# Batch 2's channel sums on GpSimd, and U and V narrowed in four places of the order

## The chip, the cores and the metric

The kernel runs on one core of a Trainium2 chip. The metric is the device time of one execution in microseconds; of several executions the median is given. The profile is of one execution; its span is the time from its first to its last instruction, and some microseconds lie outside it. The engines are TensorE (PE, with its weight loads PEld), VectorE (DVE), ScalarE (ACT), GpSimd (POOL) and SyncE (SP), which issues most of the DMAs. Each engine takes its own instructions in order.

## The reference

Attention over 4 batches of 12 heads (448 positions, 64 channels) with normed queries and keys, then two MLP layers on the 768 channels of all heads. The first layer norms its input over the channels, the second adds a product with two low-rank factors U and V.

```
def _attn_ref(q, k, v, g_q, g_k):
    q_n, k_n = (rmsnorm(q, g_q), rmsnorm(k, g_k))
    scores = np.matmul(q_n, k_n.transpose(0, 1, 3, 2)) / np.sqrt(q.shape[-1])
    scores = scores - np.max(scores, axis=-1, keepdims=True)
    attn = np.exp(scores)
    attn = attn / (np.sum(attn, axis=-1, keepdims=True) + 1e-09)
    return np.matmul(attn, v)

def _moe_ref(x, g_ln, w_ch1, w_ch2):
    mu = np.mean(x, axis=-1, keepdims=True)
    var = np.mean((x - mu) ** 2, axis=-1, keepdims=True)
    xn = (x - mu) / np.sqrt(var + 1e-06) * g_ln
    return x + np.maximum(xn @ w_ch1, 0.0) @ w_ch2

def _moe2_ref(x, U, V, w_ch1, w_ch2):
    h = x.transpose(0, 2, 1) @ U @ V
    u = x + h.transpose(0, 2, 1)
    return u + np.maximum(u @ w_ch1, 0.0) @ w_ch2
```

## The kernel before

The program has two parts, attention and MLP. Attention goes head by head, 48 heads in all; numbers of heads here count through the batches, so that batch 2 holds heads 24 to 35, and two neighbouring heads make a pair. In one turn of its loop several heads are in different phases: head n's scores (`sc`, matmuls L491 and L492 into `ps`, ScalarE's exponential L494 gives `p`), the product with the values one head behind (`pv`, L509, or L512 to L514 for the parts that are split into a high and a low half, into `po`), the row maxima two heads ahead (`mx`, matmul L455 into `pm`, VectorE's L456 gives `m`, ScalarE's L461 writes it into `ql`), the transposes of the next keys and queries (`t1`, L434 from `kk` into `pk`, copied to `a` at L437; L442 from `qd` into `pq`, copied to `bq` at L445), and the transposes of `ql` (`t2`, L469, copied to `t` at L471, which L492 reads). `kk`, `qd` and `ql` of a pair come from ScalarE's copies L312 and L315 and GpSimd's subtractions L314 and L317. SyncE's L451 moves a head's keys for the second part of the scores. VectorE's copy L523 takes a head's result to `u`, and two DMAs (L526, L527) put it into `x` and its denominators into `sum`.

A turn has four steps. In each step every task of these phases moves on by one piece, and so does the first task of a list `ln`, in which what doesn't belong to a head stands one after the other: `load_uv` from head 4 on, and after a batch's last head `scale` (loads the denominators with L537, inverts them with ScalarE's L541 and VectorE, and multiplies the six 128x448 tiles of `x` with them at L564), `ln_stats` and `ln_apply`, the norm over channels. After batch 2 come `scale`, `ln_stats` and, for the MLP's first weights, `early` and `late`, which load (`wr`), narrow (L71 and L79 on ScalarE, L83 and L87 on VectorE, result `wf`) and split weights (L945 on ScalarE, L946 on GpSimd) during the last heads. So batch 2's norm is worked on beside heads 41 to 47. The order that the program gives is rearranged by a scheduler that places instructions by times it reckons; instructions in `pin` stay in the order of the program among themselves.

`narrow` (L90 to L93) turns a 64-bit-wide input into float32: `scaled` and `bits` (ScalarE, L79 and L71), `join` and `sign` (VectorE, L83 and L87), each for every half in turn. `load_uv` (L113 to L133) calls it at L124 for U and then for V, each loaded by SyncE in two halves (L121), and then splits the factor (L127 and L129, L131 and L132).

`ln_stats` (L153) sums the six tiles of a batch over channels with four VectorE reductions of 112 columns each (L163), takes the mean over the 128 partitions with a matmul by a constant (L169), copies it to `mu` (L172), subtracts it from each tile on GpSimd (L184), squares on ScalarE (L187), adds on VectorE (L181) and takes the variance with a second matmul (L192).

The MLP follows: 4 runs (layer, pair of batches) over the columns of the weights, matmuls L1120, L1242 and L1298, each set in its order by a planner with its own costs.

Of the kernel before, what the change touches and what calls it, by code (L numbers as in the profile page):

```python
# [47 lines left out]
def build(tc, qkv, gg, g_ln, w1a, w2a, w1b, w2b, u_in, v_in, out):  # L48
    nc = tc.nc
    V, A, PL, PE = nc.vector, nc.scalar, nc.gpsimd, nc.tensor  # L50
    with ExitStack() as es:
# [37 lines left out]
        def narrow(raws, f):  # L89
            n = f.shape[1] // len(raws)  # L90
            for op in (scaled, bits, join, sign):
                for i, r in enumerate(raws):
                    op(r, f[:, i * n:(i + 1) * n])  # L93


        A.preload_act_table_set("natural_log_exp_and_others")
        ident = const([P, P], F32, "ident")
# [16 lines left out]
        def load_uv():  # L114
            for src, n, rows in ((u_in, NC * 4 * R, CP), (v_in, S, 4 * R)):
# [7 lines left out]
                yield  # L123
                narrow(parts, f)  # L124
                yield
                if rows == CP:
# [23 lines left out]

        lns, side = {}, {}

        def ln_stats(b, pool=None):  # L153
# [5 lines left out]
            lag = 2 if pool else 1  # L159
            xs = lt("xs")  # L160
            for c in range(NC):
                cs = slice(c * CP, (c + 1) * CP)
                V.tensor_reduce(xs[:, cs], x[b][:, :, cs].rearrange("p k n -> p n k"), AX.X, ALU.add)  # L163
                yield
            yield
            if pool:
                yield
            pm = side["ln"] if pool else bank("mu")
# [57 lines left out]
        def attention(ap, ep, ep2, early, late):  # L226
# [302 lines left out]

            def scale(b, q, h0, h1, pool=None):  # L530

# [21 lines left out]
                lag = 3 if pool else 2  # L553
                for n in range(len(ks) + lag):
                    if n < len(ks):
                        k = ks[n]
                        rs[k] = (f32(pool)[:, n, :] if pool else
                                 lpool.tile([P, S], F32, tag="lt", name=f"r{b}_{k}"))
                        for j in range(2):
                            q.dma_start(rs[k][j * D:(j + 1) * D, :],  # L560
                                        d[2 * k + j:2 * k + j + 1, :].to_broadcast([D, S]))
                    if n >= lag:
                        k = ks[n - lag]
                        pin(V.tensor_tensor(x[b][:, k, :], x[b][:, k, :], rs[k], ALU.mult))  # L564
                    yield
# [9 lines left out]
            for i in range(-3 - T1, NH + 2):  # L575
# [17 lines left out]
                if i - 2 in (H, 2 * H, 3 * H):  # L593
                    b = (i - 2) // H - 1
                    ln.append(scale(b, nc.sync, 0, H, xl[b] if b < 2 else None))
                if i - 2 in (H, 2 * H):
# [918 lines left out]
```

## Time and profile before

| | us |
| --- | --- |
| median of 3 runs (lowest, highest) | 1677.04 (1676.89, 1685.16) |
| the profiled execution | 1676.77 |
| its span | 1674.5 |
| TensorE busy | 1659.7 (99%) |
| VectorE busy | 1218.4 (73%) |
| ScalarE busy | 1003.2 (60%) |
| GpSimd busy | 1087.7 (65%) |
| the core's mean granted clock of TensorE | 0.997 |

The busy time of a pipelined TensorE doesn't tell that it works at its best, so the table is read for what is near its end and not for what is left. In a timeline each line has the start in us from the span's start, the duration, the engine, the line of the kernel, what is written and read, shapes, and the count where several of one kind were put together; in brackets the idle time before it and what ended it. The granted clock is a share of 2.4 GHz, so 0.5 is 1.2 GHz.

### The profile page before, as it was taken

Reading aid. Unit: us, or ns where it says so; the run is one execution under the profiler, and the core shown is the slowest. Engines: PE = TensorE matmul, PEld = TensorE weight load, DVE = VectorE, ACT = ScalarE, POOL = GpSimd, SP = SyncE. Lnnn points to the kernel's source line nnn. Section 1 sums busy time; section 2 is a strip of 40 time slices with the busy share of each in tenths; the row PEclk is TensorE's granted clock in tenths of the full one; section 3 lists DMA queues with packets and bytes.
Section 4 is the critical chain, followed back from the end, with each engine's and each line's share of the span. In section 5 each row is a group of like instructions: output and inputs, shape, how many; then the busy total and the mean of one; then the engine's idle time right before and its main releaser. Section 6 shows DMA issues by size and latency. Waiting matters only on the chain.

```text
span 1674.5 us, 24807 instructions
## 1 busy us (share of the span) xinstructions
PE 1659.7 (99%) x8251; PEld 1442.0 (86%) x8251; DVE 1218.4 (73%) x1941; ACT 1003.2 (60%) x2105; POOL 1087.7 (65%) x963
## 2 busy tenths in 40 slices
PE   8999999999999999999999999999999999999999
PEld 6676666589999999999999999999999999999998
DVE  6878787879887887866767686667667854565665
ACT  6888888767878866554544455444445534454541
POOL 5788767449767787755555587555555655776752
PEclk8999999999999999999999999999999999999999
DMA  3444445776755566544444427565657463443432
GB/s 97 117 100 116 120 117 138 200 223 199 243 173 178 180 212 200 187 141 134 152 133 158 162 83 257 187 219 179 224 192 246 169 207 116 149 151 123 149 125 76
DMA packets 134432, 273.42 MB, mean 163 GB/s; under 512 B 37280, under 2 KB 57664, under 8 KB 134304
## 3 DMA queue, kind: packets, MB, share of 16 engines
q1 hardware_dynamic: 112252, 265.24, 49.8%
q10 hardware_dynamic: 22052, 6.59, 1.7%
q8 instruction: 66, 1.08, 0.3%
q14 instruction: 62, 0.51, 0.1%
HBM read 178.80 MB, written 81.96 MB: 156 GB/s over the span
## 4 chain that ended last, share of the span: by engine, by line
PE 89%; DMA 3%; DVE 3%; issue 2%; ACT 1%; POOL 1%; SPq 0%; POOLq 0%; DVEq 0%; ACTq 0%
PE bank L1120 34%; PE bank L1298 32%; PE bank L1242 6%; PE po L509 4%; PE b L1120 2%; PE b L1242 2%; PE ps L491 2%; PE pm L455 2%; PE ps L492 1%; DVE m L456 1%; DMA raw<-in_qkv 1%; PE t L987 1%; PE xt L977 1%; PE pk L434 1%; PE pq L442 1%
## 5 line engine op out<-in xcount | busy, mean ns | idle before, releaser
L1298 PE MATMUL bank<-h,w 128*128 128x448 f32 x2655 | 586.4, 366 | 0.3 <-DVE h L1112 0.3
L1298 PEld LDWEIGHTS bank<-h,w 128*128 128x128 f32 x2655 | 497.2, 188 | 40.0 <-DVE h L1112 0.6
L1309 DVE TENSOR_TENSOR x<-x,bank 128x448 f32<-128x448 f32 x450 | 275.9, 616 | 192.9 <-PE bank L1298 188.1
L1120 PE MATMUL bank<-xh,w 128*128 128x448 f32 x1158 | 330.4, 367 | 0.0
L794 POOL TENSOR_TENSOR w<-wf,w 128x384 fp32r<-128x384 f32 x201 | 222.6, 1118 | 131.6 <-ACT w L793 131.5
L794 POOL TENSOR_TENSOR w<-s,w 128x384 fp32r<-128x384 f32 x151 | 173.8, 1154 | 155.3 <-ACT w L793 149.9
L1120 PE MATMUL bank<-T,w 128*128 128x448 f32 x1134 | 251.9, 367 | 0.0
L1120 PEld LDWEIGHTS bank<-xh,w 128*128 128x128 f32 x1158 | 216.9, 188 | 18.1 <-issue 0.8
L1120 PEld LDWEIGHTS bank<-T,w 128*128 128x128 f32 x1134 | 211.9, 188 | 16.8
L1120 PE MATMUL bank<-xl,w 128*128 128x448 f32 x579 | 211.7, 366 | 0.0
L793 ACT CAST w<-s 128x384 fp32r<-128x384 f32 x151 | 77.0, 515 | 178.5 <-PE bank L1120 166.0
L793 ACT CAST w<-wf 128x384 fp32r<-128x384 f32 x201 | 101.5, 514 | 101.2 <-PE bank L1120 82.6
L456 DVE TENSOR_REDUCE m<-pm 112x1 f32<-112x448 f32 x192 | 118.5, 619 | 46.4 <-PE pm L455 45.7
L509 PE MATMUL po<-p,vf 112*66 112x448 f32 x328 | 149.8, 539 | 0.1
L83 DVE SCALAR_TENSOR_TENSOR wf<-wf,raw 128x384 uint32<-128x384 uint32 x180 | 134.2, 752 | 10.4 <-ACT raw L71 3.8
L794 POOL TENSOR_TENSOR w<-raw,w 128x384 fp32r<-128x384 f32 x72 | 81.2, 1145 | 57.2 <-ACT w L793 57.1
L1120 PEld LDWEIGHTS bank<-xl,w 128*128 128x128 f32 x579 | 108.8, 188 | 8.7
L79 ACT ACTIVATE wf<-raw 128x384 f32<-128x384 f32 x180 | 99.3, 553 | 20.7 <-DMA raw<-in_w2a 9.5
L494 ACT ACTIVATE p<-ps 112x448 f32<-112x448 f32 x192 | 104.6, 547 | 6.2 <-PE ps L492 3.5
L1112 DVE SCALAR_TENSOR_TENSOR h<-tm,h 128x448 fp32r<-128x448 f32 x103 | 102.2, 992 | 2.8 <-ACT h L1111 2.1
L71 ACT ACTIVATE raw<-raw 128x384 uint32<-128x384 uint8 x180 | 99.9, 558 | 0.0
L1161 DVE TENSOR_TENSOR tm<-tm,bank 128x448 f32<-128x448 f32 x102 | 63.0, 617 | 47.7 <-PE bank L1120 46.8
(283 smaller groups left out, 2989.5 us busy)
## 6 DMA issues: line engine op xcount, KB each, us to landing
wd<-wf SPq DMA_DIRECT2D x94, 384.0 KB
ws<-w SPq DMA_DIRECT2D x84, 384.0 KB
w<-ws SPq DMA_DIRECT2D x84, 384.0 KB
wf<-wd SPq DMA_DIRECT2D x51, 384.0 KB
raw<-wd SPq DMA_DIRECT2D x48, 384.0 KB
raw<-in_w1b SPq DMA_DIRECT2D x48, 384.0 KB
raw<-in_w2b SPq DMA_DIRECT2D x48, 384.0 KB
raw<-in_w2a SPq DMA_DIRECT2D x44, 384.0 KB
```

Of the source, the lines that this page charges most:

```text
L71: A.activation(r[:, :, 0], r.bitcast(U8).rearrange("p n (t q) -> p n t q", t=2)[:, :, 0, 3], AF.Copy, scale=1.0 / 32, bias=-31.0 / 64)
L83: V.scalar_tensor_tensor(f, f, 3, r[:, :, 0], ALU.logical_shift_left, ALU.bitwise_or)
L456: V.tensor_reduce(m[:, c:c + 1], pm[:CP, :S], AX.X, ALU.max)
L494: A.activation(p, pb[:CP, :S], AF.Exp)
L509: PE.matmul(po[:QW, :S], vf[:, j, c, :], ps[c], start=(i == 0), stop=(i == NC - 1))
L793: job(A, 520, lambda: A.copy(form(key)[0], src()), ins, ("hi",) + key, [key])
L794: job(PL, 1100, lambda: PL.tensor_tensor(form(key)[1], src(), f32(form(key)[0]), ALU.subtract), [("hi",) + key], key, rel=rel)
L1112: soon(V, 700, lambda: V.scalar_tensor_tensor(at(*key)[:, 1], src(), 0.0, f32(at(*key)[:, 0]), ALU.max, ALU.subtract), [("hh",) + key], ke ...
L1120: PE.matmul(out[:, :S], wt[:, k, :], xt[:, k, :], start=(first and n == 0), stop=(last and n == 8), skip_group_check=True)
L1242: PE.matmul(at(*to)[:, :S], wt[:, e, :], xt, start=(m in "13" and n == 0), stop=(n == 2), skip_group_check=True)
L1298: PE.matmul(at(*key)[:, :S], wt[:, e % 3, :], t, start=(n == 0), stop=(n == 3 * G - 1))
L1309: V.tensor_tensor(x[b][:, e, :], x[b][:, e, :], at(*key)[:, :S], ALU.add)
```

## The change

`load_uv` no longer runs `narrow` in one piece. A new `narrowed` yields after each of the four operations, so the four stand in four steps of the loop.

`scale` gets a flag `add`, set for batch 2. From the step after the one that multiplies the third tile of `x`, GpSimd adds the tiles as they come: tiles 0 and 1 and then tile 2 in one step, tiles 3, 4 and 5 in a step each, into `sums[2]`. `ln_stats(2)` takes this sum, leaves its four reductions and its empty steps out, and goes to the matmul for the mean at once. The other batches sum as before.

```
--- before.py
+++ after.py
@@ -93,6 +93,13 @@
                     op(r, f[:, i * n:(i + 1) * n])
 
 
+        def narrowed(raws, f):
+            n = f.shape[1] // len(raws)
+            for op in (scaled, bits, join, sign):
+                for i, r in enumerate(raws):
+                    op(r, f[:, i * n:(i + 1) * n])
+                yield
+
         A.preload_act_table_set("natural_log_exp_and_others")
         ident = const([P, P], F32, "ident")
         make_identity(nc, ident)
@@ -121,8 +128,7 @@
                     nc.sync.dma_start(r, src[:, i * n // 2:(i + 1) * n // 2])
                     parts.append(r)
                 yield
-                narrow(parts, f)
-                yield
+                yield from narrowed(parts, f)
                 if rows == CP:
                     V.tensor_copy(u4.rearrange("p c r -> p (c r)"), f)
                     part = u4[:, :, 2 * R:3 * R]
@@ -148,7 +154,7 @@
             by(V.scalar_tensor_tensor(t, t, -0.5, a, ALU.mult, ALU.mult))
             by(V.scalar_tensor_tensor(y if to is None else to, t, 1.5, y, ALU.add, ALU.mult))
 
-        lns, side = {}, {}
+        lns, side, sums = {}, {}, {}
 
         def ln_stats(b, pool=None):
             def lt(n, pool=None):
@@ -157,14 +163,17 @@
                 return lpool.tile([P, S], F32, tag="lt", name=f"ln{b}_{n}")
 
             lag = 2 if pool else 1
-            xs = lt("xs")
-            for c in range(NC):
-                cs = slice(c * CP, (c + 1) * CP)
-                V.tensor_reduce(xs[:, cs], x[b][:, :, cs].rearrange("p k n -> p n k"), AX.X, ALU.add)
-                yield
-            yield
-            if pool:
-                yield
+            if b in sums:
+                xs = sums.pop(b)
+            else:
+                xs = lt("xs")
+                for c in range(NC):
+                    cs = slice(c * CP, (c + 1) * CP)
+                    V.tensor_reduce(xs[:, cs], x[b][:, :, cs].rearrange("p k n -> p n k"), AX.X, ALU.add)
+                    yield
+                yield
+                if pool:
+                    yield
             pm = side["ln"] if pool else bank("mu")
             pin(PE.matmul(pm[:, :S], ones_m, xs, start=True, stop=True))
             yield
@@ -527,7 +536,7 @@
                 q.dma_start(st["sum", b][h:h + 1, :], u[D:D + 1, :])
                 yield
 
-            def scale(b, q, h0, h1, pool=None):
+            def scale(b, q, h0, h1, pool=None, add=False):
 
                 def fold(d):
                     return d[h0:h1].rearrange("h s -> (h s)").rearrange("(p n) -> p n", p=P)
@@ -551,7 +560,7 @@
                 ks = range(h0 // 2, h1 // 2)
                 rs = {}
                 lag = 3 if pool else 2
-                for n in range(len(ks) + lag):
+                for n in range(len(ks) + lag + add):
                     if n < len(ks):
                         k = ks[n]
                         rs[k] = (f32(pool)[:, n, :] if pool else
@@ -559,7 +568,12 @@
                         for j in range(2):
                             q.dma_start(rs[k][j * D:(j + 1) * D, :],
                                         d[2 * k + j:2 * k + j + 1, :].to_broadcast([D, S]))
-                    if n >= lag:
+                    if add and n >= len(ks) - 1:
+                        if n == len(ks) - 1:
+                            sums[b] = xs = lpool.tile([P, S], F32, tag="lt", name=f"ln{b}_xs")
+                        for k in (1, 2) if n == len(ks) - 1 else (n - lag - 1,):
+                            PL.tensor_tensor(xs, x[b][:, 0, :] if k == 1 else xs, x[b][:, k, :], ALU.add)
+                    if lag <= n < len(ks) + lag:
                         k = ks[n - lag]
                         pin(V.tensor_tensor(x[b][:, k, :], x[b][:, k, :], rs[k], ALU.mult))
                     yield
@@ -592,7 +606,7 @@
                     ln.append(load_uv())
                 if i - 2 in (H, 2 * H, 3 * H):
                     b = (i - 2) // H - 1
-                    ln.append(scale(b, nc.sync, 0, H, xl[b] if b < 2 else None))
+                    ln.append(scale(b, nc.sync, 0, H, xl[b] if b < 2 else None, b == 2))
                 if i - 2 in (H, 2 * H):
                     ln.append(ln_stats(b, ap))
                     ln.append(ln_apply(b, ap))
```

The following pieces show the order on an engine, before and in the changed kernel; lines of the changed kernel are higher by 7 ahead of `ln_stats` and by 9 or 14 behind it.

ScalarE in the 56th to 64th us, heads 6 to 9, before; `f` is what becomes U or V (448: V), `r_0` and `r_1` its two loaded halves:

```order
L437 CAST a_8_973<-pk_968 128x448
L79 ACTIVATE f_942<-r_0_943 128x224
L494 ACTIVATE p_1_992<-ps_989 112x448
L79 ACTIVATE f_942<-r_1_945 128x224
L71 ACTIVATE r_1_945<-r_1_945 128x224
L471 CAST t_6_1003<-pt_998 66x448
L494 ACTIVATE p_2_1017<-ps_1014 112x448
L445 CAST bq_1030<-pq_1025 128x448
L290 ACTIVATE qsq_1_1033<-raw_1_814 112x512
```

The changed kernel at the same heads, from head 7's factor of the maxima, `ql`, on to the copy `kk` of pair 5:

```order
L470 ACTIVATE ql_366<-m_953 112x4
L79 ACTIVATE f_1017<-r_0_1018 128x224
L503 ACTIVATE p_0_1049<-ps_1046 112x448
L71 ACTIVATE r_0_1018<-r_0_1018 128x224
L446 CAST a_9_1063<-pk_1058 128x448
L503 ACTIVATE p_1_1076<-ps_1073 112x448
L480 CAST t_7_1087<-pt_1082 66x448
L503 ACTIVATE p_2_1100<-ps_1097 112x448
L454 CAST bq_1113<-pq_1108 128x448
L503 ACTIVATE p_3_1123<-ps_1120 112x448
L79 ACTIVATE f_1017<-r_1_1020 128x224
L321 CAST kk_1043<-raw_1_654 112x8x64
```

The last three of V's four ScalarE instructions stood between head 8's `a` and head 6's `t`; now two stand behind head 7's `ql`, and the other two beside `kk` and `qd` of pair 5.

TensorE at heads 43 to 45, before, with head 44's transposes in the second row and the mean's matmul not among the rows:

```order
L509 MATMUL po_4333<-p_1_4279,vf_354 66x448
L469 MATMUL pt_4357<-identr,ql_368 66x112 x4
L491 MATMUL ps_4365<-bq_4137,a_43_4090 112x448
L492 MATMUL ps_4365<-t_43_4290,a_362 112x448
L455 MATMUL pm_4370<-a_45_4264,bq_4308 112x448
L509 MATMUL po_4333<-p_2_4297,vf_354 66x448
L442 MATMUL pq_4374<-identr,qd_4244 128x112 x4
L491 MATMUL ps_4382<-bq_4137,a_43_4090 112x448
```

And further on, the mean's matmul of batch 2 one head later:

```order
L455 MATMUL pm_4437<-a_46_4340,bq_4379 112x448
L509 MATMUL po_4403<-p_2_4368,vf_354 66x448
L442 MATMUL pq_4441<-identr,qd_4244 128x112 x4
L169 MATMUL ln_305<-ln_xs,ones_m 128x448
L491 MATMUL ps_4449<-bq_4223,a_44_4177 112x448
L492 MATMUL ps_4449<-t_44_4362,a_364 112x448
```

In the changed kernel, from the same product with the values on:

```order
L518 MATMUL po_4339<-p_1_4282,vf_354 66x448
L478 MATMUL pt_4361<-identr,ql_368 66x112 x4
L178 MATMUL ln_305<-ln_xs,ones_m 128x448
L500 MATMUL ps_4369<-bq_4137,a_43_4090 112x448
L501 MATMUL ps_4369<-t_43_4293,a_362 112x448
L464 MATMUL pm_4374<-a_45_4264,bq_4312 112x448
L518 MATMUL po_4339<-p_2_4301,vf_354 66x448
L451 MATMUL pq_4378<-identr,qd_4244 128x112 x4
```

The mean's matmul (`ln_305<-ln_xs`) stood behind head 47's transposes L442 and now stands behind head 44's L469, 24 places of the list ahead, and reads the sum that GpSimd makes.

GpSimd at the same heads, before, with `ql` of the last pair first:

```order
L317 TENSOR_TENSOR ql_370<-raw_0_3848,qd_4244 112x8x64
L946 TENSOR_TENSOR w_277<-wf_4630,w_277 128x384
L946 TENSOR_TENSOR w_278<-wf_4630,w_278 128x384
L946 TENSOR_TENSOR w_279<-wf_4648,w_279 128x384
L946 TENSOR_TENSOR w_280<-wf_4648,w_280 128x384
L184 TENSOR_TENSOR ln_acc<-x_84,ln_mu 128x448
L184 TENSOR_TENSOR ln_sq_4497<-x_84,ln_mu 128x448
L184 TENSOR_TENSOR ln_sq_4508<-x_84,ln_mu 128x448
L184 TENSOR_TENSOR ln_sq_4521<-x_84,ln_mu 128x448
L184 TENSOR_TENSOR ln_sq_4535<-x_84,ln_mu 128x448
L184 TENSOR_TENSOR ln_sq_4552<-x_84,ln_mu 128x448
```

And in the changed kernel:

```order
L326 TENSOR_TENSOR ql_370<-raw_0_3848,qd_4244 112x8x64
L575 TENSOR_TENSOR ln_xs<-x_84 128x448
L960 TENSOR_TENSOR w_277<-wf_4625,w_277 128x384
L575 TENSOR_TENSOR ln_xs<-ln_xs,x_84 128x448 x3
L960 TENSOR_TENSOR w_278<-wf_4625,w_278 128x384
L575 TENSOR_TENSOR ln_xs<-ln_xs,x_84 128x448
L960 TENSOR_TENSOR w_279<-wf_4649,w_279 128x384
L193 TENSOR_TENSOR ln_acc<-x_84,ln_mu 128x448
```

The five additions (L575) have come in around the first two of the weights' subtractions (L946 before, L960 now), and the mean's subtractions (L184, now L193) have moved ahead of the fourth.

## Rows read from the trace of the kernel before

**Rows 1.** The table of stretches: us, busy us (count) by engine, clock, DMA share, GB/s.

```profile
10.00:16.00 6.00, 3.81 (x31) 3.06 (x29) 5.71 (x12) 5.46 (x13) 2.73 (x3) 0.94 0.35 98
16.00:26.00 10.00, 7.40 (x33) 5.85 (x34) 7.54 (x15) 6.47 (x15) 5.25 (x5) 0.52 0.10 24
...
380.00:1674.00 1294.00, 1291.02 (x6409) 1193.23 (x6407) 921.05 (x1387) 702.14 (x1410) 828.57 (x731) 1.00 0.52 172
```

**Rows 2.** Timeline of TensorE, 60 to 69 us: start, duration, instruction, idle before.

```profile
60.77 0.45 PE L492 MATMUL ps<-t,a 66*112 66x448 f32 x1
61.63 0.46 PE L455 MATMUL pm<-a,bq 128*112 128x448 f32 x1 [0.41 <-ACT bq L445]
...
68.52 0.80 PE L434 MATMUL pk<-identr,kk 112*128 112x112 f32 x4
```

**Rows 3.** Timelines of ScalarE, GpSimd and SyncE (DMA issues), 56 to 66 us.

```profile
59.60 0.40 ACT L79 ACTIVATE f<-r 128x224 f32<-128x224 f32 x1 [1.15 <-DMA r<-in_v]
...
61.05 0.53 ACT L445 CAST bq<-pq 128x448 fp32r<-128x448 f32 x1
...
64.45 1.29 POOL L314 TENSOR_TENSOR kk<-raw,kk 112x512 fp32r<-112x512 f32 x1
...
56.67 0.36 SPq L121 DMA_DIRECT2D r<-in_v  x1
```

**Rows 4.** Timeline of TensorE, heads 43 to 46 and two quiet heads before.

```profile
287.57 0.80 PE L442 MATMUL pq<-identr,qd 112*128 112x112 f32 x4
...
294.00 0.80 PE L442 MATMUL pq<-identr,qd 112*128 112x112 f32 x4
...
306.56 0.73 PE L469 MATMUL pt<-identr,ql 112*66 112x112 f32 x4
307.12 0.41 PE L491 MATMUL ps<-bq,a 128*112 128x448 f32 x1
...
308.19 0.80 PE L442 MATMUL pq<-identr,qd 112*128 112x112 f32 x4
...
316.21 0.80 PE L442 MATMUL pq<-identr,qd 112*128 112x112 f32 x4
316.85 0.99 PE L169 MATMUL ln<-ln_xs,ones_m 128*128 128x448 f32 x2
```

**Rows 5.** Timeline of VectorE, 306 to 315 us.

```profile
306.62 0.61 DVE L564 TENSOR_TENSOR x<-x,r 128x448 f32<-128x448 f32 x1
...
307.62 1.36 DVE L163 TENSOR_REDUCE ln_xs<-x 128x112 f32<-128x672 f32 x1
```

**Rows 6.** Timeline of GpSimd, 301 to 329 us.

```profile
301.02 1.67 POOL L317 TENSOR_TENSOR ql<-raw,qd 112x512 fp32r<-112x512 f32 x1
303.73 2.25 POOL L946 TENSOR_TENSOR w<-wf,w 128x384 fp32r<-128x384 f32 x1 [1.04 <-ACT w L945]
...
310.48 1.01 POOL L946 TENSOR_TENSOR w<-wf,w 128x384 fp32r<-128x384 f32 x1 [1.91 <-ACT w L945]
...
321.01 1.13 POOL L184 TENSOR_TENSOR ln_acc<-x,ln_mu 128x448 f32<-128x448 f32 x1 [0.41 <-ACT ln_mu L172]
...
324.31 4.09 POOL L184 TENSOR_TENSOR ln_sq<-x,ln_mu 128x448 f32<-128x448 f32 x3
```

**Rows 7.** Timelines of TensorE and of ScalarE, 329 to 331 us.

```profile
330.71 0.46 PE L492 MATMUL ps<-t,a 66*112 66x448 f32 x1 [0.65 <-ACT t L471]
...
329.49 0.32 ACT L541 ACTIVATE sy<-ss,tiny 128x28 f32<-128x28 f32 x1 [0.58 <-DMA ss<-sum]
```

**Rows 8.** Timeline of TensorE, the start of the span.

```profile
13.20 0.46 PE L455 MATMUL pm<-a,bq 128*112 128x448 f32 x1 [0.91 <-ACT bq L445]
...
19.21 0.74 PE L434 MATMUL pk<-identr,kk 112*128 112x112 f32 x4 [2.60 <-DVE kk L370]
```

**Rows 9.** Timeline of TensorE, the first MLP matmul and a wait in the MLP.

```profile
338.67 0.71 PE L1120 MATMUL bank<-xh,w 128*128 128x448 f32 x1
...
366.20 2.09 PE L1298 MATMUL bank<-h,w 128*128 128x448 f32 x9 [0.26 <-DVE h L1112]
```

More of the change, by code (lines that the diff above doesn't have):

```diff
@@ L93, in narrow, with narrowed @@
                     op(r, f[:, i * n:(i + 1) * n])
+        def narrowed(raws, f):
+            n = f.shape[1] // len(raws)
+            for op in (scaled, bits, join, sign):
+                for i, r in enumerate(raws):
+                    op(r, f[:, i * n:(i + 1) * n])
+                yield
         A.preload_act_table_set("natural_log_exp_and_others")
@@ L123, in load_uv @@
                 yield
-                narrow(parts, f)
-                yield
+                yield from narrowed(parts, f)
                 if rows == CP:
@@ L149, in rsqrt_newton @@
             by(V.scalar_tensor_tensor(y if to is None else to, t, 1.5, y, ALU.add, ALU.mult))
-        lns, side = {}, {}
+        lns, side, sums = {}, {}, {}
         def ln_stats(b, pool=None):
@@ L159, in ln_stats @@
             lag = 2 if pool else 1
[L160 to L163, printed above, removed]
+            if b in sums:
+                xs = sums.pop(b)
+            else:
+                xs = lt("xs")
+                for c in range(NC):
+                    cs = slice(c * CP, (c + 1) * CP)
+                    V.tensor_reduce(xs[:, cs], x[b][:, :, cs].rearrange("p k n -> p n k"), AX.X, ALU.add)
+                    yield
                 yield
-            yield
-            if pool:
-                yield
+                if pool:
+                    yield
             pm = side["ln"] if pool else bank("mu")
@@ L553, in scale @@
                 lag = 3 if pool else 2
-                for n in range(len(ks) + lag):
+                for n in range(len(ks) + lag + add):
                     if n < len(ks):
@@ L561, in scale @@
                                         d[2 * k + j:2 * k + j + 1, :].to_broadcast([D, S]))
-                    if n >= lag:
+                    if add and n >= len(ks) - 1:
+                        if n == len(ks) - 1:
+                            sums[b] = xs = lpool.tile([P, S], F32, tag="lt", name=f"ln{b}_xs")
+                        for k in (1, 2) if n == len(ks) - 1 else (n - lag - 1,):
+                            PL.tensor_tensor(xs, x[b][:, 0, :] if k == 1 else xs, x[b][:, k, :], ALU.add)
+                    if lag <= n < len(ks) + lag:
                         k = ks[n - lag]
@@ L594, in attention @@
                     b = (i - 2) // H - 1
-                    ln.append(scale(b, nc.sync, 0, H, xl[b] if b < 2 else None))
+                    ln.append(scale(b, nc.sync, 0, H, xl[b] if b < 2 else None, b == 2))
                 if i - 2 in (H, 2 * H):
```

2 lines of the change are left out of this document (1 added, 1 removed).

## The prediction

> **What bounds the kernel now.** I read the page's share of each engine first, then the table of stretches. From 380 us to the end, which is the MLP, TensorE is busy for 1291.02 of 1294.00 us at the full clock [rows 1]; its matmuls stand head to tail, nine of 448 columns in 2.09 us, and the longest wait that the timeline names there is 0.26 us [rows 9]. The order of instructions is the same from there on in both kernels. So the MLP takes what it takes, and what the change can win or lose is the moment at which TensorE is done with the attention, when its first MLP matmul starts, at 338.67 us of the span [rows 9]. The profiled execution took 1676.77 us with a span of 1674.5, so 2.3 us lie around the span; it stands 0.3 us below the median of 1677.04. There the question is where TensorE itself waits, and the timeline of its instructions answers it: each step of a head repeats every few us, so a late start shows as a longer distance between two instructions of the same kind. TensorE takes its instructions in order, hence a matmul that waits holds up all behind it.
>
> **The narrowing of U and V in four places.** Before, the eight instructions of a factor stand nearly in a row on ScalarE and VectorE. The second half of V reaches ScalarE's queue ahead of its data: at 59.60 it has idled 1.15 us for the load that SyncE issued at 56.67, so it took 2.9 us from issue to use [rows 3]. Behind it stands the copy of head 8's transposed queries, `bq`, which comes at 61.05, and TensorE's L455 waits for that: from 60.77 to 61.63 it moves 0.86 us for a matmul that takes up 0.2 us elsewhere (nine in 2.09 us [rows 9]), so 0.65 us are lost [rows 2]. In the changed order V's two L79 stand seven and fourteen places lower, behind `bq`, so this wait goes: −0.65. What is late next? V's second half now stands directly ahead of the copy `kk` of pair 5, on which GpSimd's L314 follows (64.45, 1.29 us [rows 3]), and on that head 10's transposes L434 at 68.52 [rows 2]. V's second load is now issued behind the loads of head 14's pair and into a tile that the first half's last operation (L87) must have read; the first half's operations, now a step apart, end about 63.5 by my estimate from their places among the rows of [rows 3], and with 2.9 us for the load the data are there at 66.4, `kk` at about 67.4 and L314 at about 68.8. TensorE, 0.65 earlier, wants the transposes at 67.9. So a wait of 0.9 takes the place of one of 0.65. Bounds: −0.65, if the load starts as early as before, and +1.5, if VectorE takes one 0.6 us step more on the way; I take 0, between the wait that goes and the one that comes. On SyncE that load holds up head 9's keys (L451) by some 4 us; they are read three heads later, about 19 us by the period below, and this costs nothing. The conversions and subtractions that follow (L127 to L132) feed nothing before the second layer's low-rank product and cost nothing here.
>
> **The sums of batch 2 off VectorE.** Four reductions L163, the first 1.36 us long, stand between the row maxima of heads 45 and 46 [rows 5]. The maxima come late through them, then the copies on ScalarE, then TensorE. The price shows in the period of a head, from one L442 to the next: 6.43 us in a quiet one (287.57 to 294.00) and 8.02 in the one from 308.19 to 316.21 [rows 4]. So without the reductions 8.02 − 6.43 = 1.6 us come back. Not all need come back, since VectorE also keeps other narrowing there: I bound it by −1.6 and −0.8 and take −1.6.
>
> **The sums on GpSimd, and the mean's matmul.** This is the largest term. Five additions of 128x448 now stand on GpSimd behind `ql` of the last pair, which ends at 301.02 + 1.67 = 302.69 [rows 6], with two of the weights' subtractions (L946) between them, three additions after the first and one addition after the second. The mean's matmul, L169, is on TensorE at 316.85 now; in the changed order it stands one head earlier, right behind the four transposes L469 of head 44 (306.56) and ahead of the next scores, L491 at 307.12 [rows 4]. It needs the fifth addition. When is that done? GpSimd has no addition of this form in the trace; the nearest is its subtraction L184, same shape and type, two inputs in SBUF, 1.13 us [rows 6]. L946 takes 1.01 us at 310.48 and 2.25 at 303.73, where VectorE runs instructions with two inputs [rows 6]. All free: 302.69 + 5 x 1.13 + 2 x 1.01 = 310.4. Later L184s, beside VectorE's own two-input work, took 4.09 us for three [rows 6], 1.36 or 0.23 more each. With that for the five additions and 2.25 for the first L946: 310.4 + 1.24 + 1.15 = 312.8. With 2.25 for the second one too: 314.0. I take 312.8, as the additions share GpSimd with L946 and VectorE still narrows weights there. The fifth addition also needs the last product of x with the denominators, L564, at 306.62 + 0.61 [rows 5], which is early enough. So TensorE, in order, stands from 307.1 to about 312.8: +5.7, with +3.3 and +6.9 as the bounds. Behind the waiting matmul stand the scores of head 43, the maxima's products of head 45 and everything after, so nothing of TensorE covers it: ScalarE's exponentials and VectorE's maxima have nothing to read either. No work is added on TensorE, as the matmul is only moved.
>
> The rows show that one form, L946, takes 2.25 or 1.01 us [rows 6]. Behind that the Trainium skill, SBUF — State Buffer, section "SBUF: two separate sides", puts a rule that speaks against sums on GpSimd: GpSimd and a VectorE instruction with two SBUF inputs take one shared pair of ports in turns, each for a whole instruction. By it every piece of VectorE's narrowing would be paid here, and the term would be +6.9, the sum 1.2 more; without it +3.3.
>
> **What goes after it.** At 330.71 TensorE's L492 has idled 0.65 us for a copy that stands on ScalarE behind L541, which waited 0.58 us for the transfer of the denominators (329.49) [rows 7]. That transfer starts with a copy on VectorE, no longer late by the reductions, so I count −0.65, with 0 as the other bound. At the last heads the order on ScalarE now has two exponentials behind a cast of weights; TensorE does not wait there now. Bounds 0 and +2 (about the four casts and two-input steps of 0.5 us that such an exponential would wait for), taken as 0, since TensorE is late by the wait above and the weights are not.
>
> **TensorE's clock.** The stretch table has the granted clock at 1.00 everywhere that I looked but in 10 to 16 us (0.94) and 16 to 26 us (0.52) [rows 1]. Of the two levels, 1.2 and 2.4 GHz, it was thus at the lower for 0.12 x 6 + 0.96 x 10 = 10.3 us, from about 15.3 to 25.6. Before it fell, TensorE waited for its first operands, as 0.91 us before 13.20, and was busy for 3.81 of the 6 us from 10 to 16; 2.60 us before 19.21 followed at the lower level [rows 1, 8]. I found no later wait of that size; the new one of 5.7 us would be longer than any. I therefore count on a fall. While TensorE stands it costs nothing; afterwards it costs half of the time until the clock is back. At the start that was 25.6 − 19.2 = 6.4 us, so 3.2 us is the upper bound and 0 (no fall) the lower; I take +2.0, nearer to the upper, as TensorE is denser here than at the start and may regain the clock sooner.
>
> The Trainium skill, TensorE: Matmul & The Clock Gate, section "HAM oscillation — how this bites in real kernels", has it that a TensorE which idles for long between groups of matmuls falls to its lower clock and pays for it again at each such gap. The trace agrees as far as its only fall goes; by the page the term is not 0.
>
> **The sum.** Narrowing 0; reductions −1.6; wait for the additions +5.7; denominators −0.65; tail 0; clock +2.0: +5.45 us. 1676.77 + 5.45 = 1682.2 for an execution like the profiled one, and with the 0.3 up to the median 1682.5. I say 1682, 0.3% above before. A measurement of this kernel can tell about 0.5%, 8.4 us, from no change, and the forecast lies inside that.
>
> **Rivals.** First, the wait does not become the bound: the additions run in GpSimd's idle time, or the matmul waits only shortly. Then only the gains are left, −0.65 − 1.6 − 0.65 = −2.9, which gives 1674. For it speaks that GpSimd idles 1.04 us before 303.73; against it that even with free durations the sum is done 3.3 us after TensorE asks for it. Chance 0.08. Second, the wait comes, but the clock stays up: 5.7 − 2.25 = +3.45, so 1680. For it: the one fall in the trace came after a stretch of sparse work, not after one wait. Chance 0.25. Third, on the other side, the clock's fall lasts: half speed costs half of its length, so with +3.45 from the rest it decides from a low level of 2 x (8.4 − 3.45) = 9.9 us after TensorE starts again; with the 10.3 us of the start it gives 3.45 + 5.15 = +8.6, so 1685.6. For it: this is the length that the trace has; against it: 3.9 us of that lay before TensorE was back at work. Chance 0.13. Fourth, the change is not felt at all, because the sums arrive where other work stood late anyway: 1677, chance 0.06, against the in-order place of the matmul.
>
> **How the numbers follow.** The forecast, 1682 with 1681 to 1684 about it, has 0.45, the rivals 0.08, 0.25, 0.13 and 0.06, and 0.03 is left for anything else. The range from 1676 to 1687 takes in the second and fourth and most of the third and leaves the first out. Faster by over 0.5% would be below 1668.7: the whole waiting of TensorE around the change is smaller than that, so 0.02. Slower by over 0.5% is the third rival, 0.13, and 0.01 of the rest: 0.14. Within: 0.84.
>
> **What would show it.** In the changed kernel's trace: the mean's matmul (the new L178) with an idle time of 3 to 7 us ended by GpSimd's additions, near 313 us; no reductions of batch 2 on VectorE, and head periods near 6.43 after the wait; a granted clock below 1.00 in the ten us after it; no wait for `bq` near 61 us; the first MLP matmul near 344 us instead of 338.67. I am wrong if the additions are done before TensorE arrives, if the clock does not fall, or if the distance from the first MLP matmul to the end differs from before's 1674.5 − 338.67 = 1335.8 us.

## The result, and the profile after

The changed kernel takes 1690.71 us in the median of 6 runs (1687.57 to 1696.54), the kernel before 1677.41 (1676.89 to 1685.16) in as many: slower by 0.7%, ratio 1.007 with an interval from 1.0047 to 1.0094. The profiled execution took 1691.35 us with a span of 1689.6, so 15.1 us more than before's 1674.5. Some executions of several kernels here run a part of the MLP's matmuls 2% slower, as the last section shows; the profiled one of the changed kernel did not.

Where the time came from is read from one kind of instruction that every head has. The transposes of the queries (L442 before, L451 after) start on TensorE at:

| instruction | before, us | after, us | after − before |
| --- | --- | --- | --- |
| head 8's transposes | 58.55 | 57.88 | −0.7 |
| head 9's | 65.94 | 64.03 | −1.9 |
| head 11's | 78.22 | 84.05 | +5.8 |
| head 44's | 294.00 | 301.10 | +7.1 |
| head 45's | 300.85 | 308.62 | +7.8 |
| head 46's | 308.19 | 324.31 | +16.1 |
| head 47's | 316.21 | 330.74 | +14.5 |
| first MLP matmul | 338.67 | 351.87 | +13.2 |
| last MLP matmul | 1670.66 | 1685.37 | +14.7 |

Two places carry it: 6.5 us where V is narrowed (from −0.7 to +5.8), and 6.8 us around the sums of batch 2 (7.8 to 14.5). Some 2 us came in small steps between, 1.3 went in the last heads, and 1.5 came in the MLP, most of it where one matmul waited for VectorE.

**Where V is narrowed.** TensorE's timeline of the changed kernel from 66 us on has the two waits:

```profile
70.14 0.53 PE L443 MATMUL pk<-identr,kk 112*128 112x112 f32 x4 [2.26 <-POOL kk L323]
...
75.10 0.72 PE L500 MATMUL ps<-bq,a 128*112 128x448 f32 x1 [0.86 <-DVE m L465]
```

The line that answers to [rows 2], L443 for head 10's keys, has idled 2.26 us, where before L434 came at 68.52 without a wait. Behind it, on the other engines (ScalarE, GpSimd, VectorE, SyncE):

```profile
67.78 0.40 ACT L79 ACTIVATE f<-r 128x224 f32<-128x224 f32 x1 [2.19 <-DMA r<-in_v]
...
63.03 1.77 POOL L492 TENSOR_TENSOR xl<-p,xl 112x448 fp32r<-112x448 f32 x1 [1.01 <-DVE xl L491]
...
68.82 1.27 POOL L323 TENSOR_TENSOR kk<-raw,kk 112x512 fp32r<-112x512 f32 x1 [2.02 <-ACT kk L321]
...
63.82 1.23 DVE L87 SCALAR_TENSOR_TENSOR f<-r,f 128x224 uint32<-128x224 uint32 x1
...
69.02 1.32 DVE L83 SCALAR_TENSOR_TENSOR f<-f,r 128x224 uint32<-128x224 uint32 x1 [1.31 <-ACT r L71]
70.37 1.37 DVE L87 SCALAR_TENSOR_TENSOR f<-r,f 128x224 uint32<-128x224 uint32 x1
71.78 1.36 DVE L137 CAST v<-f 128x448 fp32r<-128x448 f32 x1
...
55.20 0.80 SPq L249 DMA_DIRECT2D raw<-in_qkv  x2
...
65.13 0.35 SPq L128 DMA_DIRECT2D r<-in_v  x1
```

The load of V's second half leaves at 65.13, against 56.67 before [rows 3]; ScalarE waits 2.19 us for it, then comes the keys' copy, then GpSimd's L323. The loads of the next pair's keys (L249, at 61.33 before) now go ahead of both of V's, at 55.20. The load of the second half left late since it waits for VectorE's L87 on the first half, which ends at 65.05 (SyncE stands 2.84 us for it until then); that took 1.23 us instead of some 0.4, beside GpSimd's subtraction from 63.03 to 64.80. Afterwards three VectorE instructions, two on the second half and L137, the copy of the whole of V, take 1.3 to 1.4 us each, in step with GpSimd's, and the row maximum behind them is what TensorE waits for at 75.10. The copy has only one input, and yet it is long; before, with GpSimd idle when it started, VectorE's timeline has it as

```profile
62.02 0.38 DVE L131 CAST v<-f 128x448 fp32r<-128x448 f32 x1
```

The stretches of the same time as the long waits, in the changed kernel (columns as in [rows 1]), show the clock:

```profile
66.00:70.00 4.00, 1.89 (x6) 0.47 (x4) 2.69 (x5) 2.22 (x6) 1.98 (x2) 1.00 0.43 115
70.00:74.00 4.00, 3.85 (x21) 2.98 (x21) 3.87 (x5) 3.12 (x10) 2.88 (x3) 0.70 0.51 124
74.00:78.00 4.00, 3.14 (x10) 2.20 (x10) 3.66 (x9) 2.73 (x6) 3.31 (x4) 0.50 0.19 65
78.00:82.00 4.00, 4.00 (x13) 2.41 (x12) 1.74 (x4) 1.75 (x3) 2.90 (x3) 0.52 0.21 47
```

0.70, 0.50 and 0.52: the lower level for 0.6 x 4 + 4 + 0.96 x 4 = 10.2 us, after TensorE had been busy for 1.89 of 4 us.

**Around the sums of batch 2.** TensorE, the changed kernel:

```profile
317.82 0.71 PE L464 MATMUL pm<-a,bq 128*112 128x448 f32 x1 [3.92 <-DVE m L465]
...
320.88 1.86 PE L178 MATMUL ln<-ln_xs,ones_m 128*128 128x448 f32 x2 [0.48 <-POOL ln_xs L575]
```

The long wait, 3.92 us, is not that of the mean's matmul (0.48) but one ahead of it, at the product for head 45's maxima, and it ends with a row maximum of VectorE. VectorE's timeline, and GpSimd's beside it:

```profile
311.34 3.08 DVE L578 TENSOR_TENSOR x<-x,r 128x448 f32<-128x448 f32 x1
314.34 1.48 DVE L87 SCALAR_TENSOR_TENSOR wf<-wr,wf 128x384 uint32<-128x384 uint32 x1
315.75 1.48 DVE L83 SCALAR_TENSOR_TENSOR wf<-wf,wr 128x384 uint32<-128x384 uint32 x1
317.15 0.61 DVE L465 TENSOR_REDUCE m<-pm 112x1 f32<-112x448 f32 x1
...
318.75 0.61 DVE L578 TENSOR_TENSOR x<-x,r 128x448 f32<-128x448 f32 x1
...
308.81 1.66 POOL L326 TENSOR_TENSOR ql<-raw,qd 112x512 fp32r<-112x512 f32 x1
310.43 1.45 POOL L575 TENSOR_TENSOR ln_xs<-x 128x448 f32<-128x448 f32 x1
311.84 1.00 POOL L960 TENSOR_TENSOR w<-wf,w 128x384 fp32r<-128x384 f32 x1
312.80 4.01 POOL L575 TENSOR_TENSOR ln_xs<-ln_xs,x 128x448 f32<-128x448 f32 x3
316.77 1.31 POOL L960 TENSOR_TENSOR w<-wf,w 128x384 fp32r<-128x384 f32 x1
...
319.49 1.33 POOL L575 TENSOR_TENSOR ln_xs<-ln_xs,x 128x448 f32<-128x448 f32 x1 [1.41 <-issue]
```

From 308.81 to 318.08 GpSimd works without a break. Every VectorE instruction with two tensors from SBUF that starts in that stretch is long: the product L578 takes 3.08 us (0.61 in [rows 5]), the narrowing steps L87 and L83 1.48 each. The row maximum, whose one input comes from TensorE's result, takes 0.61 us before and after; it only stands behind them in the queue, and so TensorE waits. The additions themselves take 1.33 to 1.45 us, and L960 1.00, where L946 took 2.25 [rows 6]. So at this place GpSimd was the one that was held before, and VectorE is now. The clock again, in this stretch:

```profile
312.00:318.00 6.00, 2.08 (x10) 1.13 (x11) 6.00 (x5) 1.02 (x3) 5.84 (x5) 0.94 0.31 86
318.00:324.00 6.00, 5.52 (x13) 2.85 (x14) 3.02 (x7) 3.59 (x9) 2.40 (x3) 0.50 0.77 239
```

### The profile page after: what moved, and what is told of

It is laid out like the page before. It is cut to its first block, busy times and chain, and to the rows that moved or that the text cites. A ratio compares the mean times of both kernels' runs of the same rounds, so it can differ in the third digit from the quotient of the medians.

```text
span 1689.6 us, 24810 instructions
## 1 busy us (share of the span) xinstructions
PE 1666.0 (99%) x8251; PEld 1445.3 (86%) x8251; DVE 1226.0 (73%) x1937; ACT 1004.2 (59%) x2105; POOL 1090.3 (65%) x968
## 4 chain that ended last, share of the span: by engine, by line
PE 85%; DVE 6%; DMA 3%; ACT 2%; issue 2%; POOL 1%; SPq 0%; ACTq 0%; DVEq 0%; POOLq 0%
PE bank L1134 32%; PE bank L1312 31%; PE bank L1256 6%; PE po L518 4%; PE b L1134 2%; PE b L1256 2%; PE ps L500 2%; PE pm L464 1%; PE ps L501 1%; DVE m L465 1%; DMA raw<-in_qkv 1%; DMA tm<-xn 1%; PE t L1001 1%; PE xt L991 1%; ACT p L503 1%
## 5 line engine op out<-in xcount | busy, mean ns | idle before, releaser
L83 DVE SCALAR_TENSOR_TENSOR wf<-wf,raw 128x384 uint32<-128x384 uint32 x180 | 134.3, 753 | 13.3 <-ACT raw L75 4.6
```

The source lines that it names most:

```text
L83: V.scalar_tensor_tensor(f, f, 3, r[:, :, 0], ALU.logical_shift_left, ALU.bitwise_or)
```

## The experiments

The theory after this look: (a) U's slower narrowing lets the loads of the next pair's keys ahead of V's and takes a buffer, so V's second half comes late; (b) GpSimd's back-to-back instructions hold VectorE's two-input instructions, that is, make them wait, and through the row maxima TensorE; (c) after either wait TensorE's clock falls and that costs again. The rivals are in the expectations. The ratio of each run is to runs of the kernel before taken beside it (medians 1675.77 to 1677.00 us). How far behind a head or the first MLP matmul is below is always against before, by the starts in the table.

### The two parts alone

In e1 the narrowing is as in the change and the sums as before, in e5 the other way round.

```
e1:  narrow(parts, f); yield   ->  yield from narrowed(parts, f)      # and no more
e5:  the changed kernel with   narrow(parts, f); yield
```

> Only the narrowing of U and V is spread over four places; the sums of batch 2 stay on VectorE. Theory (buffers and clock): TensorE waits 2.8 us for head 10's keys near 70 us, the clock is at its lower level for about ten us after it, and the first MLP matmul comes about 6 us later than before: 1683. Rival (the two parts only cost together, by meeting in the scheduler's order): no loss here, 1677.

> Only the sums of batch 2 are moved to GpSimd; U and V are narrowed in one piece. Theory (the additions hold VectorE's two-input instructions): a product of x with the denominators takes about 3 us on VectorE instead of 0.6, two narrowing steps 1.5 instead of 0.55, TensorE waits about 4 us for a row maximum, the clock falls after it; first MLP matmul 6 us later, 1683. Rival (the loss in these heads came from what the narrowing had shifted): about 1676.

e1: 1681.93 us, 1.0029 (1.0015 to 1.0044); e5: 1693.36, 1.0086 (1.0061 to 1.0112). Each part costs by itself, and neither rival holds; e5's time is 10 us above the expected 1683. In e1 TensorE's timeline has the wait of the changed kernel again, and the table of stretches the fall of the clock, though a shorter one:

```profile
70.67 0.52 PE L440 MATMUL pk<-identr,kk 112*128 112x112 f32 x4 [2.25 <-POOL kk L320]
...
70.00:74.00 4.00, 3.33 (x15) 2.63 (x16) 3.90 (x4) 3.34 (x11) 3.39 (x3) 0.66 0.31 62
74.00:78.00 4.00, 3.58 (x17) 2.30 (x16) 3.97 (x10) 2.85 (x8) 2.97 (x3) 0.92 0.43 122
```

The lower level lasts 0.68 x 4 + 0.16 x 4 = 3.4 us here and 10.2 in the changed kernel, after waits of 2.25 and 2.26 us, in the same order of TensorE's instructions. From head 8 to head 11 e1 loses 3.8 us and the changed kernel 6.5: 2.7 us apart, where half of the 6.8 us would be 3.4; 0.4 of the 2.7 is the second wait, which is shorter in e1 (0.42 against 0.86). That is the nearest thing to a price of the clock in these runs. First MLP matmul of e1: 343.50, 4.8 behind.

In e5 there is the same wait for a maximum as in the changed kernel, a longer one for the sum, and one more at the first MLP matmul (TensorE's timeline):

```profile
310.38 0.46 PE L465 MATMUL pm<-a,bq 128*112 128x448 f32 x1 [3.93 <-DVE m L466]
...
313.43 1.86 PE L179 MATMUL ln<-ln_xs,ones_m 128*128 128x448 f32 x2 [1.28 <-POOL ln_xs L576]
...
347.97 0.68 PE L1135 MATMUL bank<-xh,w 128*128 128x448 f32 x2 [2.37 <-DVE u L533]
```

First MLP matmul 9.3 behind; with e1's 4.8 that is 14.1, near the 13.2 of both parts together. Of the 17.4 us by which e5's span is longer, 7.7 came in the MLP, by the slower pace of the last section and a clock of 0.72 from 348 to 354 us behind that third wait, so its total says less than the stage does.

### Which factor, and the buffers

```
e2, e3:  if rows == CP: (U)  yield from narrowed(parts, f)  /  narrow(parts, f); yield
         else:          (V)  narrow(parts, f); yield        /  yield from narrowed(parts, f)
e4, e10: r = (rpool.tile(...) if rows == CP else
              lpool.tile([rows, n // 2, 2], U32, tag="lt", ...))
e10:     pin(nc.sync.dma_start(r, ...))
```

> U is narrowed in four places, V in one piece as before. Theory: it is U's later end that lets the next pair's loads go ahead of V's and into the free buffers, so V's second half still comes late: the same wait and fall of the clock as with both spread, about 1683. Rival (V's own four steps are what makes its second half late): no loss, 1676 to 1677.

> V is narrowed in four places, U in one piece. Theory: V's loads keep their place ahead of the next pair's, no wait near 70 us, 1676 to 1678. Rival (V's own steps make it late): about 1683.

> Both spread as in the change, but V's two halves are loaded into tiles of their own and not into the ring of four that the pairs' keys use. Theory: no wait for V's load any more, no fall of the clock, first MLP matmul at or slightly ahead of before's 338.67 us, 1676 to 1677. Rival (the place of V's instructions on ScalarE ahead of the copy of the keys is the cost, not the load): the wait at head 10's keys stays near 2 us, 1681 to 1683.

> Both factors spread, sums on VectorE; V's halves in tiles of their own, and their loads kept behind the pair's loads instead of at the start of the span. Theory (the ring of buffers makes V's second half late): it arrives near 60 us, no wait of 2 us at head 10's keys, clock 1.00 from 26 to 120 us, head 11 within 1 us of before's. Rival (the narrowing's place ahead of the copy of the keys on ScalarE is enough): a wait of 1 to 2 us stays and the clock falls.

e2: 1676.38 us, 1.0005 (0.9987 to 1.0023); e3: 1678.38, 1.0013 (0.9999 to 1.0027). By the times neither is told from before, and e2's expected 1683 is missed. By the traces the theory's split holds: with U alone TensorE waits at head 10's keys again, and the clock is at 0.74 from 70 to 74 and 0.84 from 74 to 78 us; with V alone that wait is not there, only three of 0.63 to 0.68 us, two of them near 61 us, like before's in [rows 2]. In e2:

```profile
70.51 0.52 PE L444 MATMUL pk<-identr,kk 112*128 112x112 f32 x4 [1.82 <-POOL kk L324]
```

At head 11 e2 is 2.5 us behind before and e3 1.2, so U alone brings a part of e1's 3.5; at the first MLP matmul they are 1.8 and 0.5 behind.

e4 was to take the ring of buffers out. It did (no wait at head 10's keys, clock 1.00 from 40 to 120 us) and took 1685.35, 1.0049 (1.0034 to 1.0064): V's loads then need no buffer, went to the very start of the span among the first heads' loads, and head 0's keys came late (3.41 us of wait at 14.00 against 0.36 at 11.40). That was another loss than the one on trial, 3.0 us by head 3, so e10 keeps the loads behind the pair's. There V's halves arrive together, `kk` is not late, the clock stays at 1.00, and the theory's main point holds:

```profile
67.07 0.46 PE L462 MATMUL pm<-a,bq 128*112 128x448 f32 x1 [1.15 <-DVE m L463]
...
70.38 0.46 PE L498 MATMUL ps<-bq,a 128*112 128x448 f32 x1 [0.60 <-DVE m L463]
...
64.81 1.67 DVE L83 SCALAR_TENSOR_TENSOR f<-f,r 128x224 uint32<-128x224 uint32 x2
...
66.94 2.33 DVE L87 SCALAR_TENSOR_TENSOR f<-r,f 128x224 uint32<-128x224 uint32 x2
```

But 1.15 and 0.60 us of waits for row maxima are there instead: the two L83 together take 1.67 us and the two L87 2.33, beside GpSimd. Head 11 is 1.7 behind before, more than the 1 expected. Late loads were thus one cause, VectorE held beside GpSimd the second. The time, 1682.52, 1.0038 (1.0027 to 1.0050), is not explained by this: in the profiled execution the first MLP matmul is only 0.3 behind, and 7.2 us came in the MLP, at its slower pace.

### Who holds whom around the sums

```
e6:  V.tensor_tensor(xs, ...)          in place of PL.tensor_tensor(xs, ...)
e7:  PL.tensor_tensor(xs, ..., x[b][:, k, :], ALU.add)
     PL.tensor_tensor(xs, xs, x[b][:, k, :], ALU.add)        # once more
e11: for n in range(len(ks) + lag + 5 * add):
         if add and n >= len(ks) + lag:   k = n - len(ks) - lag + 1
e12: as e11, the tiles added in the order 0, 5, 1, 2, 3, 4
```

All four narrow U and V in one piece, as e5 does.

> As the sums alone, but the same five additions are made by VectorE (0.6 us each, 3.0 in place of the reductions' 5.4). Theory: GpSimd holds VectorE no longer, the product takes 0.6 us, no wait of 4 us and no fall of the clock: 1675 to 1677. Rival (the mean's matmul one head earlier, or the shift of other work, is what costs): still over 1680.

> As the sums alone, but each tile but the first is added twice by GpSimd (ten additions, so the mean is that of another sum). Theory: VectorE is held about twice as long; TensorE's waits in heads 43 to 46 sum up to 9 to 12 us instead of about 5, and the time is 4 to 8 us above that of the sums alone. Rival (the additions hide beside other work and something else made VectorE late): within 2 us of the sums alone.

> Only the sums of batch 2 on GpSimd, at the same place of GpSimd's order as in the change, but the mean's matmul 18 places later on TensorE. Theory (VectorE is held by the additions): its product still takes about 3 us and the wait for a row maximum stays near 4 us, the wait for the sum (1.3 us) goes. Rival (the early place of the mean's matmul is the cost, as the prediction had it): both waits go, first MLP matmul at 338 to 340.

> As the one before, with the same order on TensorE and VectorE, but the additions begin with tile 5, so that GpSimd makes all five behind the last product and behind the first two subtractions of the weights. Theory: the products take 0.6 us again, what is held are one or two narrowing steps of the weights, the wait of 4 us falls to under 1.5 us, the clock stays at 1.00, first MLP matmul at 337 to 340. Rival (it is the sums' number on GpSimd, not where they meet VectorE's two-input steps): a wait of 3 us or more somewhere in heads 43 to 47.

e6: 1679.06 us, 1.0002 (0.9990 to 1.0013), two us above the expected range and below the rival's. With the same five additions on VectorE the loss is gone, and no wait is over 1.72 us; nothing is won on before either, probably since the additions stand in VectorE's way as the reductions did.

e7: 1694.53, 1.0101 (1.0079 to 1.0122), TensorE's timeline:

```profile
310.44 0.71 PE L465 MATMUL pm<-a,bq 128*112 128x448 f32 x1 [3.94 <-DVE m L466]
...
319.73 1.86 PE L179 MATMUL ln<-ln_xs,ones_m 128*128 128x448 f32 x2 [6.71 <-POOL ln_xs L577]
```

The time is 1.2 us above e5's where 4 to 8 were expected; the first MLP matmul, which leaves the MLP's pace out, is 6.4 behind e5's. The sum of the waits, 10.65 us, is as the theory said, but not its reason: VectorE is held as in e5 (3.09, 1.48, 1.48 us; e5: 3.08, 1.48, 1.48) and the wait for the maximum, 3.94, is the same. What grew is the time until the sum is there. So VectorE is held by the GpSimd instructions that meet its own, not by how many stand in the queue.

e11 and e12 tell the wait for the sum from the hold. In e11 GpSimd's order is that of the change and only the mean's matmul stands 18 places later; in e12 the order on TensorE and VectorE is e11's, and only GpSimd's additions come later, behind the last product. e11: 1686.59, 1.0070 (1.0053 to 1.0087):

```profile
308.03 0.70 PE L465 MATMUL pm<-a,bq 128*112 128x448 f32 x1 [3.94 <-DVE m L466]
```

The matmul for the mean no longer waits, and the 3.94 us for the maximum stay: the place of the mean's matmul was not the cause. The time again holds over 3 us of the MLP's slower pace; the first MLP matmul is 2.8 behind. e12: 1677.49, 1.0009 (0.9998 to 1.0021), TensorE, VectorE and GpSimd:

```profile
312.98 0.45 PE L465 MATMUL pm<-a,bq 128*112 128x448 f32 x1 [0.54 <-DVE m L466]
...
314.65 1.02 PE L179 MATMUL ln<-ln_xs,ones_m 128*128 128x448 f32 x2 [0.26 <-POOL ln_xs L576]
...
303.21 0.61 DVE L579 TENSOR_TENSOR x<-x,r 128x448 f32<-128x448 f32 x1
...
309.62 1.35 DVE L83 SCALAR_TENSOR_TENSOR wf<-wf,wr 128x384 uint32<-128x384 uint32 x1 [1.20 <-ACT wr L71]
311.01 1.38 DVE L87 SCALAR_TENSOR_TENSOR wf<-wr,wf 128x384 uint32<-128x384 uint32 x1
...
303.38 4.85 POOL L961 TENSOR_TENSOR w<-wf,w 128x384 fp32r<-128x384 f32 x2 [1.04 <-ACT w L960]
...
309.42 5.18 POOL L576 TENSOR_TENSOR ln_xs<-ln_xs,x 128x448 f32<-128x448 f32 x4
```

The products are back at 0.61 us, the two L961 take 4.85 as before, only two narrowing steps (1.35 and 1.38) meet the additions, and the wait is 0.54 us. The clock is 1.00 from 306 to 342 us and the first MLP matmul 0.7 behind before. Five additions on GpSimd cost nothing in themselves; what cost was that they met VectorE's products and narrowing while row maxima stood behind these.

### The clock

```
in pv, head 5's last product:      for _ in range(24 / 11): PE.matmul(ln, ones_m, ones_m)
in mx, head 45, second product:    for _ in range(36 / 16): PE.matmul(ln, ones_m, ones_m)
```

> The changed kernel with 24 and 36 matmuls of 128 columns (0.11 us each) that nobody reads, put on TensorE just ahead of its two long waits, so that it works while it would stand. Theory: the waits for data end as late as in the changed kernel, but the clock does not fall, and 5 to 7 us come back: first MLP matmul about 345 instead of 351.5, 1684. Rival (the low clock costs little because other engines are the bound there): within 1.5 us of the changed kernel, 1690.

> As the filled kernel, with 11 and 16 of the matmuls that nobody reads (0.23 us each, so 2.5 and 3.7 us, about the two waits) in place of 24 and 36. Theory: TensorE's clock stays up after both places; head 11 stands about 2.5 us behind before's where the changed kernel stood 5.8 behind, and the first MLP matmul comes 5 to 7 us earlier than the changed kernel's 351.9. Rival (the low clock costs little): within 2 us of 351.9.

Both failed to give back what was expected: 1693.88 us, 1.0104 (1.0077 to 1.0130), and 1692.35, 1.0104 (1.0084 to 1.0125); first MLP matmul 356.76 and 352.69, so later than the changed kernel's 351.87. In e8 the matmuls were too many: in the trace one takes 0.23 us, twice what I had reckoned, so in the first place they covered 5.3 us where a wait of 2.26 was to be filled. The clock was at 1.00 from 62 to 90 us, and head 11 was still 5.0 us behind. In the second place the clock fell behind them all the same: 0.90, 0.50 and 0.75 in the three stretches of 6 us from 318 us on. In e9 the number was right, but TensorE's timeline shows the wait moved:

```profile
70.20 0.52 PE L443 MATMUL pk<-identr,kk 112*128 112x112 f32 x4 [0.86 <-POOL kk L323]
...
74.76 0.57 PE L503 MATMUL ps<-bq,a 128*112 128x448 f32 x1 [2.40 <-DVE m L468]
```

The wait for the keys is down to 0.86 us, and the one for VectorE's maximum, 0.86 in the changed kernel, is 2.40, and then the clock fell all the same (0.62 and 0.95 in the two stretches of 4 us from 74 on). That maximum starts on VectorE at 74.08, in the changed kernel at 74.44, behind the same three held steps, so part of the low clock was probably hidden behind VectorE. In the second place of e9 the wait for the maximum is down to 0.36 us, the sum is waited for 1.64, and the clock fell for 3.5 us (0.94 and 0.77 from 312 to 324) in place of 6.7. Head 47 comes 2.9 us ahead of the changed kernel's, but the first MLP matmul 0.8 behind it, after two more waits for maxima, 0.53 and 1.30 us.

The two runs are no clean test either, since the scheduler also placed other instructions elsewhere: two products with the values that stand ahead of head 10's key transposes in the changed kernel stand behind them in e8 and e9. What the low clock costs by itself is not settled by these two runs.

## Why the prediction was wrong

The terms gave +5.45 us, the profiled executions +15.1. Around the sums of batch 2 the terms −1.6, +5.7 and +2.0 gave 6.1 and 6.8 were measured, though by another mechanism than the one forecast. What took the time out of the range is the narrowing, 6.5 us where 0 was taken, with some 2 us of small steps between the places and 1.5 in the MLP that had no term.

- **What bounds the kernel:** right. The place of the first MLP matmul tells nearly all (13.2 of 14.7 us); 1.5 us were added in the MLP, by a wait for VectorE's result at 705 us above all, which I had not counted.
- **The narrowing, taken as 0 with +1.5 as the bound:** this step failed. Its mechanism, V's second half late and with it `kk`, was named and came, and so did the gain: no wait for `bq` is left near 61 us, and head 9 is 1.9 us ahead. But the size was wrong: TensorE was done at 67.9, as forecast, and stood until 70.14, a wait of 2.26 us in place of 0.9. I had let the first half end at 63.5; VectorE's L87 started only at 63.82 and, held by GpSimd, ended at 65.05. Then I priced only the wait: neither the clock nor the three held steps at 69 to 73 us were in the bounds. Measured: +6.5 from head 8 to head 11.
- **The reductions, −1.6:** the number came, from head 46 to head 47 the changed kernel takes 6.43 us in place of 8.02. That the missing reductions are the reason is not shown: e6 and e12, also without them, take 7.90 and 8.70 us there, e6 with the additions on VectorE, e12 with the mean's matmul and two held narrowing steps in that stretch.
- **The wait for the sum, +5.7:** wrong. The mean's matmul waited 0.48 us, 1.28 in e5. TensorE was held earlier, for 3.92 us, by a row maximum. The step that failed is the sentence that took GpSimd as the one that pays: I had L946 at 2.25 us for the price of two engines meeting, and lengthened GpSimd's instructions. I did not price the other direction, VectorE waiting for GpSimd, though before's trace has it: VectorE's timeline there, beside GpSimd's L317 of [rows 6], has

```profile
301.47 1.63 DVE L87 SCALAR_TENSOR_TENSOR wf<-wr,wf 128x384 uint32<-128x384 uint32 x1
...
303.56 0.61 DVE L564 TENSOR_TENSOR x<-x,r 128x448 f32<-128x448 f32 x1
304.09 0.55 DVE L87 SCALAR_TENSOR_TENSOR wf<-wr,wf 128x384 uint32<-128x384 uint32 x1
304.56 0.55 DVE L83 SCALAR_TENSOR_TENSOR wf<-wf,wr 128x384 uint32<-128x384 uint32 x1
```

  1.63 us against 0.55 for one form; the last three lines run at their free times while L946 is the one that waits. The waits measured, 3.92 + 0.48, are near the 5.7 by chance. So is the time of the sum: the fifth addition ended 10.4 us behind `ql`, forecast were 10.1. GpSimd's own work was shorter than taken (9.1 us), but the addition begins only right behind VectorE's last product, at 318.75, after 1.41 us without work; the prediction had called that product early enough.
- **The rule on the shared ports:** the Trainium skill, SBUF — State Buffer, section "SBUF: two separate sides", has the pair go to whichever starts first, for a whole instruction. The traces agree as far as single instructions go: a VectorE step of 1.48 us is its own 0.55 and the rest of a GpSimd addition of 1.33. I quoted the rule and applied one half of it. That a product which stands ready lets three of GpSimd's instructions go first, 3.08 us, is what the trace adds.
- **The clock, +2.0:** the fall came, in both places, for 10.2 us in the first and 6.7 in the second (0.94 and 0.50 in the two stretches shown). I counted one, and with +2.0 some 4 us of it. Of 1.2 GHz for 17 us at most 8.5 us would be lost; the difference to e1 speaks for a cost, e8 and e9 leave open how much of it other waits hide.
- **Denominators, −0.65, and tail, 0:** from head 47 to the MLP 1.3 us came back in the changed kernel; in e5, e7, e11 and e12 a wait of 1.00 to 2.43 us came right before the first MLP matmul, up to a little above the bound of +2. Whether the two exponentials named for the tail bring it is not shown.
- **The rivals:** the one on the other side, the clock, gave 1685.6 and had 0.13; the time went beyond it. Missing was a rival in which VectorE is the one held, and in which both places cost at once.

None of the versions beats the kernel before: e2, e3, e6 and e12 are level with it.

## What to carry to other kernels

When work goes from VectorE to GpSimd, price both directions of their meeting: look for VectorE's two-input instructions, and its copies, beside GpSimd's in the trace, and ask what stands behind them in VectorE's queue. Work moved to an idle engine is free only where its operands do not compete with the engine that others wait for; putting the same additions a few microseconds later took the loss away. Where an instruction is spread or moved, follow the loads and buffers that go with it, since another load may take the free buffer.

## What the runs showed of the hardware

VectorE and GpSimd hold each other in both directions, and for more than one instruction. Where GpSimd had a queue of ready instructions, a VectorE product waited for three of them (3.08 us against 0.61), and then the two took turns, 1.48 us for each of VectorE's steps of 0.55. Where VectorE came first, in the kernel before, its product at 303.56 and the two narrowing steps behind it ran at 0.61, 0.55 and 0.55 us, and GpSimd's L946, from 303.73 on, took 2.25 against 1.00. VectorE's copy of V, with one input, took 1.36 us beside GpSimd's L305 (71.45 to 72.88) against 0.38 before.

TensorE's lower clock lasted 10.2 us after one wait of 2.26 us and 3.4 after another of 2.25, with the same instructions on TensorE in the same order.

The MLP's matmuls have two paces at the full clock, which I had not known of. The stretch from 600 to 690 us of the changed kernel, and of e5:

```profile
600.00:690.00 90.00, 90.00 (x446) 83.40 (x445) 72.25 (x98) 56.87 (x111) 68.31 (x57) 1.00 0.65 208
```

```profile
600.00:690.00 90.00, 90.00 (x437) 81.75 (x436) 71.78 (x96) 56.86 (x112) 68.02 (x56) 1.00 0.63 203
```

TensorE is busy for all 90 us at 1.00 in both, and does 446 and 437 matmuls. What sets this pace is open; it came in the profiled executions of e4, e5, e7, e10 and e11 for some 180 to 360 us.
